# Adding spectral products on VectorE instead of TensorE in a two-layer SSM and GEGLU kernel, with a reordered opening

## The chip, the cores and the metric

The kernel runs on one core of a Trainium2 chip. The metric is the device time of one launch in microseconds (us). A core has five engines that run their own instruction lists and wait for each other through semaphores: TensorE (PE, with its weight loads shown as PEld), VectorE (DVE), ScalarE (ACT), GpSimd (POOL) and SyncE (SP). In this kernel the last two mostly issue DMA transfers; POOL also does small per-row statistics.

## The reference

One sequence of S = 2048 tokens with D = 576 features goes through two layers. Each layer has a gated long convolution (A) and a GEGLU feed-forward block (B), both with the same weights in both layers.

```python
def _A_ref(q, k, v, shift_k, ssm_k, ssm_D):
    ...                                   # k_shift: 4-tap causal filter of k
    kv = k_shift * v
    ...                                   # y: causal convolution of kv with ssm_k over 2048 tokens, by FFT
    y = y + kv * ssm_D[None, None, :]
    return q * y
def _B_ref(x, w_gate, w_up, w_down):
    return (_gelu(x @ w_gate) * (x @ w_up)) @ w_down    # 576 -> 4608 -> 576
x = A_q
x = x + _A_ref(_layernorm(x, axis=-1), A_k, A_v, A_shift_k, A_ssm_k, A_ssm_D)
x = x + _B_ref(_layernorm(x, axis=-1), B_w_gate, B_w_up, B_w_down)
x = x + _A_ref(_layernorm(x, axis=-1), A_k, A_v, A_shift_k, A_ssm_k, A_ssm_D)
x = x + _B_ref(_layernorm(x, axis=-1), B_w_gate, B_w_up, B_w_down)
```

The convolution depends on k, v and the filters alone, not on x. Its result y is computed once and used by both layers, as a gate on the normalised x.

## The kernel before

**Feed-forward part.** The tokens are cut into four chunks of 512 (c = 0 to 3), each of four tiles of 128 rows. A unit is a pair (layer, chunk). The units run in the order (0,0), (0,1), (1,0), (1,1), (0,2), (0,3), (1,2), (1,3), numbered 0 to 7, and are grouped in passes [0], [1,2], [3,4], [5,6], [7] (L711). A pass goes three times through a third of the 4608 hidden columns, for each of its units; one such step is called a visit here, and there are 24. A visit has 12 gate-up groups (L1087: 18 matmuls each of 64 rows by 512 columns into one PSUM pair from a pool of three; ACT takes the Gelu, L1091; DVE multiplies it with the up half into hT, L1092) and then four down groups (L1103: 24 full-array matmuls of 288 columns each; DVE adds the result to x_c, L1132 or L1137).

Before its first visit a unit's input has to be gated with y (L855 and L862, with row statistics on POOL, L819 to L835, and a square with row sum on ACT, L827), normalised (L888 and L890, tile xn) and transposed by DMA from SP's queue into xnT (L918, two transfers for each of the four tiles). Unit 0's input is transposed on PE in the opening instead (`turn0`, L1002).

**Convolution part.** It is done by blocks of 512 tokens in a frequency domain of 512 points, in four tiles of 128 frequencies (kt = 0 to 3) with two parts each, 0 and 1. H are the transformed filter blocks, K the transformed kv blocks. Block m of the result needs the products K[a] * H[m-a] for a = 0 to m. Each of them takes, for each kt and part, a multiplication (`prod`, L222 or L225) and a subtraction or addition (L226) on DVE, and gives a bf16 tile `sum` of 128 by 576. Blocks 1, 2 and 3 have 16, 24 and 32 such products. `accumulate` (L229) adds them up on PE: each product is the moving operand of two matmuls of 288 columns with an identity as weights, and the sum stands in PSUM (cps). For kt < 2 ACT copies it to an f32 tile eo (L391). For kt >= 2 `both` (L235) makes the sum and the difference of that tile and the PSUM one (L240), and `shifted` (L243, L245) combines these with the block before into z. Four inverse transforms (L258) then give the tiles of y. The forward transform of a kv block is L205, with ACT copies into eo (L208) and DVE sums (L213). The kv block itself is made by L160 to L170. K and H blocks are kept in DRAM (Kd, Hd): they are spilled by POOL's DMAs (L263) and read back into kr and hr buffers (L316, L324).

**What sets the order.** All lists are in program order. A planner in the kernel (`Pace`, with one constant per operation, L30 to L37, and `fill`, L973) places the convolution work among the visits while the program is built: after each gate-up group and within the down groups it takes operations from two VectorE queues, one of the convolution (`run_v`, L443) and one of gates and norms (`run_vq`), as long as its own clocks leave room, and PE's convolution work (`run_p`, L460). `hurry()` (L1049) is true until block 1's last inverse is placed. As long as it is, the convolution's queue goes first and PE's convolution work may stand between gate-up groups; later gates and norms go first, and that PE work stands within down groups only. `conv.spills` holds POOL's small operations and spills with the time from which they may be placed.

**The opening** (`begin`, L472) makes the DFT tables, the four H blocks in 16 tiles (`h_tile`, L567; matmuls L184, eviction by ACT L186, spill L263), block 0 of the convolution and unit 0's input. Most of H's tiles pass through the `hr` buffers, four before; the order of its last part is written out by hand (from L641).

Of the kernel before, what the change touches and what calls it, by code (L numbers as in the profile page):

```python
# [12 lines left out]
ALU = mybir.AluOpType  # L13
# [41 lines left out]
class Conv:  # L55
# [9 lines left out]
    def __init__(self, tc, ctx, pace, A_k, A_v, A_shift_k, A_ssm_k, A_ssm_D, ident, psp, cpsp, ypool):  # L65
# [10 lines left out]
        self.krp = pool("c_kr", 3)  # L76
        self.hrp = pool("c_hr", 4)
# [4 lines left out]
        self.eop = pool("c_eo", 2)  # L82
        self.kvp = pool("c_kv", 1)
# [15 lines left out]
        self.U = deque()  # L99
        self.kr_free, self.hr_free = [0.0] * 3, [0.0] * 4  # L100
        self.npr = self.nkr = self.nhr = 0
        self.V, self.L, self.Pq = deque(), deque(), deque()
        self.spills = deque()

# [167 lines left out]
    def step(self, m, kv=None, loaded=False):  # L272
# [37 lines left out]
        def load(kt, a):  # L310
            def run():
                if a < m:
                    kr[(kt, a)] = (self.nkr % 3, self.krp.tile([P, 2, D], BF16, tag="kr", name="kr"))
                    self.kr_free[self.nkr % 3] = NEVER
                    self.nkr += 1
                    nc.gpsimd.dma_start(out=kr[(kt, a)][1][:].rearrange("p s d -> p (s d)"), in_=self.Kd[a][kt])  # L316
                if m == 1 and a == 0:
                    hr[(kt, a)] = (None, self.H1[:, kt, :, :])
                    at[("ld", kt, a)] = t.pe + 8.0
                    return  # L320
                hr[(kt, a)] = (self.nhr % 4, self.hrp.tile([P, 2, D], BF16, tag="hr", name="hr"))
                self.hr_free[self.nhr % 4] = NEVER
                self.nhr += 1
                nc.gpsimd.dma_start(out=hr[(kt, a)][1][:].rearrange("p s d -> p (s d)"), in_=self.Hd[m - a][kt])  # L324
                at[("ld", kt, a)] = t.pe + 8.0
            return run
        for kt, a in pairs:
            self.L.append((lambda a=a: max(self.hr_free[self.nhr % 4] if (m, a) != (1, 0) else 0.0,
                                           self.kr_free[self.nkr % 3] if a < m else 0.0),
                           load(kt, a)))  # L330
# [25 lines left out]
        def v(kt, a, part):  # L356
            def run():
                K = kc[kt] if a == m else kr[(kt, a)][1]
                slot = self.npr % N_SM
                prs[(kt, a, part)] = (slot, self.prod(part, K, hr[(kt, a)][1]))  # L360
                self.pr_free[slot] = NEVER

# [7 lines left out]
                return fin  # L370
            return run
        for kt, a in pairs:
            for part in range(2):
                keys = [("ld", kt, a)] + ([("kc", kt % 2, s, h) for s in range(2) for h in range(2)] if a == m else [])
                self.V.append((lambda g=get(*keys): max(g(), self.pr_slot()), C_PR, v(kt, a, part)))
        st = {}

# [32 lines left out]
        for kt in range(2):  # L410
            for s in range(2):
                for h in range(2):
                    self.Pq.append((lambda: max(get("kv")(), NEVER if self.neo > 1 else 0.0), 0.49, fwd(kt, s, h)))
        for kt in KTS:
            for part in range(2):
                for a in range(m + 1):
                    need = get(("pr", kt, a, part))
                    self.Pq.append(((lambda need=need: max(need(), NEVER if self.neo > 1 else 0.0)) if kt < 2 and a == m
                                    else need, 0.245, acc(kt, part, a)))
# [23 lines left out]
    def run_v(self, limit):  # L443
# [9 lines left out]
        if r > t.pe + 0.2 or max(t.dve, t.pe - 1.0) + cost > limit:  # L453
            return False
        self.V.popleft()
        fin = run()
        fin(t.on_dve(cost, r))
# [13 lines left out]

    def begin(self, gate0, norm0, turn0, x0_stats, more, scratch, wide, stay):  # L472

        tc, nc, D = self.tc, self.nc, self.D
        with ExitStack() as es:
# [176 lines left out]
            inv0(3)  # L652
            nc.scalar.activation(out=warm[:], in_=self.pis[:, 1:2], func=ACT.Gelu_apprx_tanh)
            more(2)
# [27 lines left out]
            h_tile(3, 3, self.hrp)  # L682
# [6 lines left out]
def ssm_geglu_kernel(ctx, tc, A_q, A_k, A_v, A_shift_k, A_ssm_k, A_ssm_D, B_x, B_w_gate, B_w_up,  # L689
# [126 lines left out]
    def mean_after(v, when):  # L816
        def run():
            v["nm"] = small.tile([P, 1], F32, tag=v["pfx"] + "nm", name="nm")
            nc.gpsimd.tensor_scalar(out=v["nm"][:], in0=v["s"][:], scalar1=-1.0 / D, scalar2=None, op0=ALU.mult)  # L819
            v["nm_at"] = max(t.pe, when) + C_TINY  # L820
        conv.spills.append((when, run))

    def square_task(get_x, v):
        def run():
# [6 lines left out]
            def root():  # L831
# [4 lines left out]
                v["rstd_at"] = max(t.pe, when) + 2 * C_TINY  # L836
            conv.spills.append((when, root))
        aq.append((at_v(v, "nm_at"), C_SQ, run))
# [150 lines left out]
    with tc.manual_schedule():  # L989
# [11 lines left out]

        def turn0(j, act):  # L1002
            if 0 not in xnT_of:
# [3 lines left out]
            for b in range(NKC):  # L1007
                c0 = b * P if b < 5 else HK + (b - 5) * P
                nc.tensor.transpose(pt[:, b // 5, (b % 5) * P:(b % 5 + 1) * P], xn0[j][:, c0:c0 + P], ident[:])
            (nc.scalar.copy if act else nc.vector.tensor_copy)(  # L1010
                out=xnT_of[0][:, 5:NKC, tok], in_=pt[:, 1, 0:4 * P].rearrange("p (b q) -> p b q", q=P))
            nc.scalar.copy(out=xnT_of[0][:, 0:5, tok], in_=pt[:, 0, 0:5 * P].rearrange("p (b q) -> p b q", q=P))
# [3 lines left out]
        def gate0(j):  # L1016
# [3 lines left out]
            aq.pop()[2]()  # L1020
            conv.spills.pop()[1]()

        def more(k):
# [7 lines left out]
            else:  # L1031
                load_x(1)
        conv.begin(gate0, norm0, turn0, lambda k: [run() for _, _, run in g0[4 * k:4 * k + 4]], more,
                   lambda dt: xtp.tile([P, RT if dt == I32 else 2, D], dt, tag="xnT", name="ang"),
# [19 lines left out]
        for wb, ph, ui, first, final in visits:  # L1054
# [25 lines left out]
            for fi in range(FP):  # L1080
# [13 lines left out]
                if gi == FG - 1 and final:  # L1094
                    when_due(t.pe + (FP - FG) * C_GU + 12.0, load_wgu, n + 3)
                fill(t.pe + C_GU + LEAD, hurry(), hurry())
            for j in range(RT):
# [17 lines left out]
                for fi in range(FP):  # L1115
# [76 lines left out]
```

## Time and profile before

| | us |
|---|---|
| Median of three runs | 977.12 (976.35 to 979.27) |
| The profiled execution, its own time | 973.51 |
| Its span, first to last instruction | 971.7 |
| PE busy in it | 949.8 (98%) |
| DVE busy in it | 537.3 (55%) |
| ACT busy in it | 305.4 (31%) |
| First gate-up matmul | 65.82 |

The profile is one execution, in which each instruction has its start and duration. A row of groups names the source line, engine, operation, output and inputs, the shape and count, then the busy time and the mean of one in ns, then the engine's idle time just before these instructions and what ended it. The chain is the work that ended last, followed back from the last instruction. A row of stretches gives the length and each engine's busy time in it. An engine that is not on the chain may be idle for free, and its time counts only where another engine waits for it.

### The profile page before, as it was taken

The numbers are of one execution on the slowest core, as the hardware profiler recorded it, in microseconds if no ns is written. First come the engines' busy times: TensorE is split into PE (matmuls) and PEld (weight loads), VectorE is DVE, ScalarE is ACT, GpSimd is POOL, SyncE is SP. The second block draws the span as 40 slices with busy tenths as digits, with TensorE's granted clock in tenths as the row PEclk, the third lists the DMA queues.
The fourth block names the chain that finished last, engine by engine and source line by source line (L and its number), as shares of the span: only waits on it lengthen the run. The fifth ranks groups of instructions, "written<-read, shape, count | busy, mean of one in ns | idle before, by whom it ended". The sixth has DMA issues, their size and how long they took to land.

```text
span 971.7 us, 19304 instructions
## 1 busy us (share of the span) xinstructions
PE 949.8 (98%) x8256; PEld 547.9 (56%) x8256; DVE 537.3 (55%) x973; ACT 305.4 (31%) x559; POOL 139.5 (14%) x303
## 2 busy tenths in 40 slices
PE   8989999879999999999999999999999999999998
PEld 5755554536556465565565565565565466466455
DVE  8957887858498555879543333564323324533332
ACT  7765213522221533414113322233212213411211
POOL 2353100512020301413000000231000001200000
PEclk9999999989999999999999999999999999999999
DMA  7989975955680740497360270385360450398730
GB/s 180 307 227 291 271 171 134 181 150 123 128 281 22 152 121 14 110 209 189 81 155 16 45 148 30 74 145 125 68 152 1 88 133 1 54 239 170 158 77 26
DMA packets 129067, 127.48 MB, mean 131 GB/s; under 512 B 45588, under 2 KB 121685, under 8 KB 128981
## 3 DMA queue, kind: packets, MB, share of 16 engines
q1 hardware_dynamic: 119904, 90.85, 44.4%
q0 software_dynamic: 8944, 34.49, 11.0%
q8 instruction: 64, 1.05, 0.5%
q10 hardware_dynamic: 132, 0.91, 0.3%
q14 instruction: 23, 0.18, 0.1%
HBM read 105.58 MB, written 10.62 MB: 120 GB/s over the span
## 4 chain that ended last, share of the span: by engine, by line
PE 92%; DVE 4%; DMA 3%; ACT 1%; issue 0%; POOL 0%; ACTq 0%; SPq 0%; DVEq 0%
PE gu L1087 58%; PE dn L1103 28%; PE cps L232 2%; PE cps L258 1%; PE cps L205 1%; DMA k<-in_A_k_dram 1%; DMA xnT<-xn 1%; DMA Hd<-h 1%; DVE kvt L160 1%; PE ps L184 0%; DVE prod L225 0%; DVE yb L226 0%; DVE kvt L165 0%; PE ps L258 0%; DVE stats L771 0%
## 5 line engine op out<-in xcount | busy, mean ns | idle before, releaser
L1087 PE MATMUL gu<-xnT,wgu 64*128 64x512 bf16 x5184 | 568.2, 377 | 7.9 <-DMA xnT<-xn 7.9
L1087 PEld LDWEIGHTS <-wgu 64*128 64x128 bf16 x5184 | 251.4, 94 | 314.8 <-issue 19.3
L1092 DVE TENSOR_TENSOR hT<-ga,gu 128x512 bf16<-128x512 f32 x288 | 197.7, 687 | 282.4 <-ACT ga L1091 281.1
L1091 ACT ACTIVATE ga<-gu 128x512 f32<-128x512 f32 x288 | 171.9, 597 | 545.0 <-PE gu L1087 541.9
L1103 PE MATMUL dn<-wd,hT 128*128 128x288 bf16 x2304 | 297.4, 286 | 0.5 <-DVE ob L1112 0.5
L1103 PEld LDWEIGHTS <-hT 128*128 128x128 bf16 x2304 | 223.3, 98 | 66.4 <-issue 10.5
L1137 DVE TENSOR_TENSOR x_c<-x_c,dn 128x576 f32<-128x576 f32 x64 | 48.2, 753 | 83.2 <-PE dn L1103 82.8
L819 POOL TENSOR_SCALAR nm<-s 128x1 f32<-128x1 f32 x60 | 20.6, 343 | 370.4 <-DVE x_c L1132 160.2
L827 ACT ACTIVATE junk<-x_c,nm 128x576 bf16<-128x576 f32 x48 | 36.9, 769 | 22.2 <-POOL nm L819 22.1
L835 POOL TENSOR_TENSOR rstd<-ve,neghalf_t 128x1 f32<-128x1 f32 x60 | 36.9, 614 | 5.0
L226 DVE TENSOR_TENSOR sum<-prod 128x576 bf16<-128x576 bf16 x72 | 33.0, 458 | 2.7
L184 PEld LDWEIGHTS <-G 128*128 128x128 bf16 x256 | 25.9, 102 | 14.6 <-issue 5.7
L184 PE MATMUL ps<-h,G 128*128 128x288 bf16 x192 | 27.8, 299 | 4.2 <-ACT h L186 3.0
L324 POOL DMA_DIRECT2D hr<-Hd x32 | 17.4, 543 | 73.5 <-DVE prod L225 73.4
L1123 DVE TENSOR_TENSOR ob<-x_c,dn 128x576 bf16<-128x576 f32 x15 | 11.3, 754 | 29.4 <-PE dn L1103 18.4
L834 POOL TENSOR_SCALAR ve<-ss 128x1 f32<-128x1 f32 x60 | 17.7, 296 | 64.8 <-ACT junk L827 64.6
L316 POOL DMA_DIRECT2D kr<-Kd x24 | 13.7, 572 | 85.2 <-DVE prod L225 85.2
L232 PE MATMUL cps<-sum,ident 128*128 128x288 bf16 x144 | 25.3, 287 | 0.0
L160 DVE TENSOR_TENSOR kvt<-k,skc 128x1152 bf16<-128x1152 bf16 x32 | 23.9, 754 | 1.8 <-DMA k<-in_A_k_dram 1.2
L213 DVE TENSOR_TENSOR kc<-eo 128x288 bf16<-128x288 f32 x48 | 19.4, 452 | 2.7 <-ACT eo L208 2.6
L208 ACT COPY eo<-cps 128x576 f32<-128x576 f32 x24 | 15.3, 636 | 16.1 <-PE cps L205 11.9
L266 POOL DMA_DIRECT2D out_dram<-ob x12 | 6.7, 561 | 88.9 <-DVE ob L1123 88.9
(115 smaller groups left out, 471.3 us busy)
## 6 DMA issues: line engine op xcount, KB each, us to landing
wgu<-in_B_w_gate_dram SPq DMA_DIRECT2D x45, 576.0 KB, 5.8
wd<-in_B_w_down_dram SPq DMA_DIRECT2D x30, 864.0 KB, 7.3
wgu<-in_B_w_up_dram SPq DMA_DIRECT2D x45, 512.0 KB, 7.7
hr<-Hd POOLq DMA_DIRECT2D x32, 288.0 KB, 5.5
kr<-Kd POOLq DMA_DIRECT2D x24, 288.0 KB, 4.6
Hd<-h POOLq DMA_DIRECT2D x12, 288.0 KB, 4.2
Kd<-kc POOLq DMA_DIRECT2D x12, 288.0 KB, 8.1
k<-in_A_k_dram POOLq DMA_DIRECT2D x3, 1008.0 KB, 12.2
```

What stands on the lines that cost most here:

```text
L160: nc.vector.tensor_tensor(out=st[dst][:], in0=self.kt_[b][:, s0:s0 + 2, :], in1=self.skc[:, j, :].unsqueeze(1).to_broadcast([P, 2, D]), op ...
L184: nc.tensor.matmul(ps[:, h, 0:HW], lhsT=G[:, i, s * NFQ + kt * P: s * NFQ + (kt + 1) * P], rhs=src[:, i, h * HW:(h + 1) * HW], start=(i == ...
L226: nc.vector.tensor_tensor(out=dst, in0=pr[:, 0, :], in1=pr[:, 1, :], op=ALU.subtract if part == 0 else ALU.add)
L232: nc.tensor.matmul(ps[:, h, 0:HW], lhsT=self.ident[:], rhs=pr[:, h * HW:(h + 1) * HW], start=first, stop=last)
L819: nc.gpsimd.tensor_scalar(out=v["nm"][:], in0=v["s"][:], scalar1=-1.0 / D, scalar2=None, op0=ALU.mult)
L827: nc.scalar.activation(out=junk[:], in_=get_x(), func=ACT.Square, bias=v["nm"][:, 0:1], accum_out=v["ss"][:])
L835: nc.gpsimd.tensor_tensor(out=v["rstd"][:], in0=ve[:], in1=neghalf_t[:, 0:1], op=ALU.pow)
L1087: nc.tensor.matmul(pair[:, s, :], lhsT=w[r0:r0 + HK, k, gi * P:(gi + 1) * P], rhs=xnT[r0:r0 + HK, b, :], start=(k == 0), stop=(k == NKC - 1))
L1091: nc.scalar.activation(out=ga[:], in_=pair[:, 0, :], func=ACT.Gelu_apprx_tanh)
L1092: nc.vector.tensor_tensor(out=hT[:, fi, :], in0=ga[:], in1=pair[:, 1, :], op=ALU.mult)
L1103: nc.tensor.matmul(acc[:, h, 0:HW], lhsT=hT[:, fi, j * P:(j + 1) * P], rhs=wd[2 * wb + fi // WT][:, fi % WT, h * HW:(h + 1) * HW], start=( ...
L1137: nc.vector.tensor_tensor(out=xh, in0=xh, in1=acc[:, :, 0:HW], op=ALU.add)
```

## The change

For blocks 2 and 3 the identity matmuls go. The first product of each kt and part is written as f32 into a tile `zs` from the eo pool, each further one is added to it by an f32 `tensor_tensor` on DVE, and the sum and difference are then made from two such tiles in SBUF, without an ACT copy. Block 1 stays as it was. The pool of `sum` tiles shrinks from six to four, that of hr from four to three, and that of eo grows from two to four.

The order changes in three places. The convolution's VectorE queue goes first only until block 1's own operations are done (`conv.left`), where it was until its last inverse is placed. POOL's statistics may be placed two units of the planner's time earlier (`AHEAD`), at a smaller booked cost (`C_TINY`). In the opening the Gelu table is loaded earlier, and the gates of tiles 0, 2 and 1 and their statistics come before the H tiles that follow, with the last step of the statistics split off as `root0`; all four of unit 0's transposes are now evicted half by DVE and half by ACT.

```diff
-C_SQ, C_TINY = 0.85, 1.0
-N_KC, N_SM = 4, 6
+C_SQ, C_TINY = 0.85, 0.6
+N_KC, N_SM, N_EO, N_HR = 4, 4, 4, 3
+C_AC, C_AB = 0.65, 0.8
+AHEAD = 2.0
...
         def v(kt, a, part):
             def run():
                 K = kc[kt] if a == m else kr[(kt, a)][1]
+                if m > 1 and a == 0:
+                    sums[(kt, part)] = self.eop.tile([P, 2, HW], F32, tag="eo", name="zs")
+                    self.prod(part, K, hr[(kt, a)][1], sums[(kt, part)][:].rearrange("p h d -> p (h d)"))
+                else:
...
+        def add(kt, a, part):
+            def run():
+                slot, pr = prs[(kt, a, part)]
+                f = sums[(kt, part)]
+                nc.vector.tensor_tensor(out=f[:], in0=f[:], in1=self.halves(pr[:]), op=ALU.add)
...
+        def cross(kt, part):
+            def run():
+                b = self.both(kt, part, sums[(kt, part)][:], sums[(kt + 2, part)][:])
...
+                if m > 1:
+                    self.V.append((lambda: 0.0, C_AC, add(kt, a, part)))
+                    if a == m and kt >= 2:
+                        self.V.append((lambda: 0.0, 2 * C_AB, cross(kt - 2, part)))
+                        self.V.append((lambda: 0.0, 2 * C_TB, shift(kt - 2, part)))
...
-        for kt in KTS:
+        for kt in KTS if m == 1 else ():
             for part in range(2):
                 for a in range(m + 1):
...
             pair0(1, 0)
+            nc.scalar.activation(out=warm[:], in_=self.pis[:, 1:2], func=ACT.Gelu_apprx_tanh)
             h_tile(1, 1, self.hrp)
...
             inv0(3)
-            nc.scalar.activation(out=warm[:], in_=self.pis[:, 1:2], func=ACT.Gelu_apprx_tanh)
...
             gate0(0)
             gate0(2)
+            root0(0)
+            root0(2)
+            gate0(1)
+            root0(1)
             h_tile(2, 2, self.hrp)
+            norm0(0)
             h_tile(2, 1, self.hrp)
-            gate0(1)
-            norm0(0)
+            gate0(3)
+            root0(3)
+            norm0(2)
+            turn0(0)
             h_tile(2, 3, self.hrp)
-            turn0(0, True)
-            gate0(3)
-            norm0(2)
+            turn0(2)
+            norm0(1)
             h_tile(3, 0, self.hrp)
-            turn0(2, True)
-            norm0(1)
+            turn0(1)
+            norm0(3)
             kv1_ops(2)
             h_tile(3, 2, self.hrp)
-            norm0(3)
-            turn0(1, False)
-            kv1_ops(2)
+            turn0(3)
+            kv1_ops(6)
             h_tile(3, 1, self.hrp)
-            turn0(3, False)
-            kv1_ops(4)
             h_tile(3, 3, self.hrp)
...
-        conv.spills.append((when, run))
+        conv.spills.append((when - AHEAD, run))
...
         conv.step(1, kv=conv.kv1[8:], loaded=True)
+        conv.left = len(conv.V)
...
-                fill(t.pe + C_GU + LEAD, hurry(), hurry())
+                fill(t.pe + C_GU + LEAD, hurry(), conv.left > 0)
...
-                        fill(t.pe + 1.5, True, hurry())
+                        fill(t.pe + 1.5, True, conv.left > 0)
```

More of the change, by code (lines that the diff above doesn't have):

```diff
@@ L371, in v, with fin, shift, run @@
             return run
+        sums = {}
+        def add(kt, a, part):
[3 more added lines that the diff above has]
+                nc.vector.tensor_tensor(out=f[:], in0=f[:], in1=self.halves(pr[:]), op=ALU.add)
+                def fin(when):
+                    self.pr_free[slot] = when
+                return fin
+            return run
+        def cross(kt, part):
+            def run():
+                b = self.both(kt, part, sums[(kt, part)][:], sums[(kt + 2, part)][:])
+                for sg in range(2):
+                    nyb[(part, kt, sg)] = b[sg]
+                return lambda when: None
+            return run
+        def shift(kt, part):
+            def run():
+                for sg in range(2):
+                    z[(part, kt, sg)] = self.yb[(1 - part, kt, sg)]
+                    self.shifted(nyb[(part, kt, sg)], z[(part, kt, sg)], part)
+                return lambda when: mark(("z", kt, part), when + LAG)
+            return run
+        eo_done = get(*[("kc", kt, s, h) for kt in range(2) for s in range(2) for h in range(2)])
         for kt, a in pairs:
@@ L455, in run_v @@
         self.V.popleft()
+        self.left -= 1
         fin = run()
@@ L836, in root @@
                 v["rstd_at"] = max(t.pe, when) + 2 * C_TINY
-            conv.spills.append((when, root))
+            conv.spills.append((when - AHEAD, root))
         aq.append((at_v(v, "nm_at"), C_SQ, run))
@@ L1032, in more @@
                 load_x(1)
-        conv.begin(gate0, norm0, turn0, lambda k: [run() for _, _, run in g0[4 * k:4 * k + 4]], more,
+        conv.begin(gate0, root0, norm0, turn0, lambda k: [run() for _, _, run in g0[4 * k:4 * k + 4]], more,
                    lambda dt: xtp.tile([P, RT if dt == I32 else 2, D], dt, tag="xnT", name="ang"),
```

37 lines of the change are left out of this document (21 added, 16 removed).

## The prediction

> **What bounds the kernel now.** I read the page first (the chain by engine), then who TensorE waited for, then the chain in order of time, then stretches of the run.
>
> ```profile
> span 971.7 us, 19304 instructions
> ...
> PE 92%; DVE 4%; DMA 3%; ACT 1%; issue 0%; POOL 0%; ACTq 0%; SPq 0%; DVEq 0%
> ```
> ```profile
> PE gu L1087 <- DMA xnT<-xn: 7.9, 1, 7.9
> ```
> TensorE (PE) is the bound: 92% of the chain. Its only long wait is one of 7.9 us for the transposed input xnT of unit 1. It never waits for the gate product hT that VectorE (DVE) makes. So an instruction taken off PE shortens the run by its own spacing, unless something else becomes late.
>
> ```profile
> 544.18 23.41 PE gu L1087 x216
> 567.60 11.87 PE dn L1103 x96
> ```
> ```profile
> 146.60:191.60 45.00, 44.57 (x379) 25.49 (x378) 36.34 (x75) 20.23 (x38) 11.46 (x26) 1.00 0.70 152
> 191.60:199.50 7.90, 0.01 (x2) 0.04 (x2) 0.78 (x3) 0.00 (x0) 1.26 (x4) 0.80 1.15 272
> 199.50:238.70 39.20, 39.20 (x330) 21.63 (x332) 31.27 (x62) 12.10 (x24) 10.81 (x22) 0.95 0.54 133
> 199.50:506.90 307.40, 307.40 (x2688) 176.75 (x2690) 209.16 (x389) 90.36 (x168) 52.27 (x108) 0.99 0.55 129
> 276.10:314.90 38.80, 38.80 (x343) 22.55 (x344) 33.21 (x58) 8.07 (x14) 3.73 (x7) 1.00 0.35 122
> 430.70:468.50 37.80, 37.80 (x335) 21.77 (x336) 32.16 (x64) 11.57 (x22) 9.59 (x20) 1.00 0.76 186
> 544.20:579.50 35.30, 35.30 (x314) 19.77 (x316) 11.26 (x16) 12.82 (x28) 3.82 (x12) 1.00 0.55 103
> ```
> The second fence gives the spacing: 96 full-array matmuls of 288 columns in 11.87 us, 0.1236 us each. The third has one visit (one unit, one third of its hidden columns) to a row; its columns are length, then PE, PEld, DVE, ACT and POOL busy, granted clock, DMA share, GB/s. A visit with no convolution matmuls takes 35.30. The visit from 430.7 has 20 identity matmuls by the program's order and takes 2.5 more, 0.125 each: they sit among matmuls of their own shape and cost just their spacing.
>
> **The change part by part.**
>
> 1. *Identity matmuls removed.* Block 2 makes 24 products and block 3 makes 32, each added by two matmuls: 112. At 0.1236 us that is **-13.8 us**, all on the path. Nothing of it was hidden: in those visits PE is busy for the whole length.
>
> 2. *Adds on VectorE.* Eight of each block's products are now written in f32, and the other 40 each get an f32 add.
>
> ```profile
> L1092 DVE TENSOR_TENSOR hT<-ga,gu 128x512 bf16<-128x512 f32 x288 | 197.7, 687 | 282.4 <-ACT ga L1091 281.1
> ...
> L226 DVE TENSOR_TENSOR sum<-prod 128x576 bf16<-128x576 bf16 x72 | 33.0, 458 | 2.7
> ...
> L240 DVE TENSOR_TENSOR yb<-eo,cps 128x576 bf16<-128x576 f32 x24 | 17.0, 748 | 3.1 <-PE cps L232 3.0
> ...
> L222 DVE TENSOR_TENSOR prod<-kr,hr 128x1152 bf16<-128x1152 bf16 x20 | 15.0, 751 | 0.0
> ```
> No row has an all-SBUF f32 add of 576 elements. It lies between the bf16 form, 0.458, and the f32 form with one PSUM side, 0.748. I take 0.748, because its element size is that of the add: 40 x 0.748 = 29.9, and 16 x (0.748 - 0.458) = 4.6 for the f32 products, so DVE gets +34.5 us (18.3 at the low end). The 16 L240 operations stay and read SBUF; 8 ACT copies go, and ACT, with 1% of the chain, is no bound.
>
> Does it fit beside PE? The eight visits from 199.5 to 506.9 (307.4 us, the row above) hold 209.2 us of DVE work. They shrink to about 292 and then hold 244, 84% on average. The densest visit by the order of the changed program is the eighth: 12 hT products (8.2), 11 convolution products (each 0.751 for the multiplication and 0.458 for the sum or difference, 13.3, and 0.9 for three f32 forms), 8 adds (6.0) and 8 other f32 operations of 576 (at 0.748, 6.0) are about 34 us in 35.3, some 96%. The densest before were 33.21 of 38.80 (86%) and 32.16 of 37.80 (85%), without one PE wait on hT. The cover is three PSUM pairs: a late hT product stops PE only once it is over one gate-up group late. The planner books 0.65 for an add that I price at 0.748, so DVE falls behind its plan by 0.1 per add, 4 us over all, in two dense stretches. Below, nothing; above, those 4 us in full. I take **+1.0 us**, nearer to the rows that show no wait.
>
> 3. *Unit 1's gates first.* This aims at the 7.9 us.
>
> ```profile
> 189.58 9.22 DMA xnT<-xn
> ```
> ```profile
> 174.75 0.42 PE L1103 MATMUL dn<-wd,hT 128*128 128x288 bf16 x2
> ```
> ```profile
> 189.36 0.57 DVE L888 TENSOR_SCALAR xn<-x_c,nm,rstd 128x576 bf16<-128x576 f32 x1
> ```
> ```profile
> 183.19 11.48 SPq L918 DMA_TRANSPOSE xnT<-xn  x6
> ```
> Today the last normalised tile is made at 189.4, waits behind four other transposes on SP's queue, and has landed 9.2 us later, when PE has been through with unit 0 since 191.6. In the changed program VectorE's list leaves the convolution at the end of block 1: three tiles are normalised, and their six transposes issued, before this visit's down stage, and the fourth stands right behind the first down group (24 matmuls from 174.75, so 177.7, then 0.8 for its residual add and 0.8 for the norm: 179.5). SP has no weight load between these transposes. With the same 9.2 it lands at 188.7; PE needs it at 191.3. So the wait goes, with 2.6 us to spare, and so does what follows it: the visit at 199.5 took 39.20 where 35.30 and 16 matmuls of 0.12 make 37.2, at a granted clock of 0.95. Together 7.9 + 2.0 = **-9.9 us**; nothing if it stays. Next late would be unit 2's input, but its last transposes stand 14 us of PE work ahead of its use. The nm operations now go to POOL up to 2 us early, where they hold back the kr and hr loads queued behind them by at most as much.
>
> ```profile
> hr<-Hd POOLq DMA_DIRECT2D x32, 288.0 KB, 5.5
> kr<-Kd POOLq DMA_DIRECT2D x24, 288.0 KB, 4.6
> ```
> The planner books 8 us for these loads (a constant of the code), and they land in 5.5 and 4.6: the rest covers it, and I cost it at nothing; without that cover VectorE would wait those 2 us.
>
> 4. *The opening.* The Gelu table load moves ahead, the gates of tiles 0, 2 and 1 come first, and the H buffers shrink from four to three.
>
> ```profile
> 45.95 1.28 ACT L653 ACT_TABLE_LOAD   x1
> ...
> 58.86 1.19 ACT L186 ACTIVATE h<-ps 128x576 bf16<-128x576 f32 x2 [1.03 <-DMA Hd<-h]
> ```
> ```profile
> 51.92 6.86 DMA Hd<-h
> ...
> 63.42 0.50 PE xps L1009 x9
> 63.92 0.98 PE cps L184 x8
> ...
> 65.88 4.20 PE gu L1087 x37
> ```
> ```profile
> 50.81 1.14 PE L184 MATMUL cps<-h,G 128*128 128x288 bf16 x8 [1.65 <-ACT h L186]
> ```
> Tile (2,0) is spilled at 51.92 and lands at 58.8; only then can ACT evict the tile four places on, and PE runs without pause from 59.56 to the gates at 65.88. With three buffers the same landing releases the tile *three* places on, (2,3). The table load (1.28) no longer stands before the squares, but a third gate's statistics now go to POOL ahead of the spill: I take its issue at 50.9, one earlier. PE: from about 51.1 a transpose (0.50), two half tiles (0.98 each), a transpose and a half tile, to 55.1; then it waits. Landing 50.9 + 6.86 = 57.8, two evictions 1.2, PE again at 59.0; seven half tiles and two transposes are left, 7.9: gates at 66.9, **+1.1 us**. If the landing doesn't move (the DMA engines are what is full there), +2.1; if it takes the 2.4 of the later spills, no pause is left and the gates start at 55.1 + 7.9 = 63.0, -2.9.
>
> ```profile
> DMA to landing us min/median/max: 6.8/6.8/6.9
> ```
> ```profile
> DMA to landing us min/median/max: 2.4/2.4/2.4
> ```
> These are the two spills from 51.9, and that of 64.4. I take the first, being at the same place.
>
> The pause from 55.1 to 59.0 is longer than any in the opening now (1.65), all of which kept clock 1.00; the 7.9 pause was followed by 0.95 and a loss of 2.0. [...]
>
> **Sum.** -13.8 + 1.0 - 9.9 + 1.1 = -21.6 us. The profiled execution took 973.51 (span 971.7 and 1.8 around it) and would take 951.9. The median of the runs is 977.12, 3.6 above it; the same difference gives **955.5 us**.
>
> **The rivals.**
>
> - *The transposes still come late* (a slow landing, or DVE late with the fourth norm): 9.9 is not won: 965.4. For: only 2.6 us to spare, at DMA shares up to 1.15. Against: three of four tiles are long through. 0.11.
> - *VectorE late in the dense visits, mildly*: all 4 us of the planner's error and some late inverses, 6 in place of 1: 960.5. 0.12.
> - *VectorE becomes the bound, and the kernel slower.* Place: the seven visits of blocks 2 and 3 that hold adds, 84 gate-up groups, each with its hT behind an add in VectorE's queue. If each stopped PE by an add (0.748) it would cost 62.8, less 22.6: 1017. It decides from 22.6 / 84 = 0.27 us per group on. For: 96% busy. Against: no wait on hT at 86%, and the three PSUM pairs. 0.04.
> - *The clock falls in the opening's pause*: 2.0 more by the visit at 199.5: 957.5. [...] 0.10.
> - *The matmuls leave and PE waits instead*, say for weights, so that nothing is gained: 977. PE is busy over whole visits at DMA shares near 0.5. 0.02.
>
> **How the numbers follow.** My forecast, with small deviations, has 0.61; it is the likeliest. Lowest: no loss on VectorE and -2.9 in the opening, 977.1 - 26.6 = 950.5; with the runs' scatter of about one below the median, 949.5. The range reaches up over the mild rival, the clock and the late transposes, to 966; left out are the rest of these and the last two, about 0.12. About 0.3% (3 us) is what a measurement of this kernel tells from no change. Faster: 0.61 + 0.11 + 0.12 + 0.10 = 0.94; same 0.02; slower 0.04.
>
> **What would show it.** Step 1: 32 identity matmuls left, the fourth, fifth and eighth to tenth visits at 35.3 to 36. Step 2: the add's row near 750 ns, and no PE wait on hT over 1 us. Step 3: the wait on xnT gone from PE's list and clock 1.00 in the visit behind it. Step 4: one PE pause near 4 us, ended by ACT behind an Hd landing, gates starting near 67. I am wrong if PE lists many waits on hT, if the adds run far over 750 ns, or if a later unit's xnT wait appears.

## The result, and the profile after

The changed kernel took 953.67 us (median of four runs, 952.37 to 953.76) against 977.0 for the kernel before (976.35 to 979.27): a ratio of 0.9754, with a 95% interval from 0.9736 to 0.9772. 955.5 had been forecast, with a range of 949.5 to 966. The profiled execution is the one of 952.37, with a span of 950.6.

First the page of the changed kernel, then who PE waited for (us in total, times, longest), its head and seven of its rows:

```profile
span 950.6 us, 19103 instructions
...
PE 934.6 (98%) x8144; PEld 537.8 (57%) x8144; DVE 568.8 (60%) x1015; ACT 299.1 (31%) x549; POOL 141.0 (15%) x303
...
PE 92%; DVE 4%; DMA 2%; POOL 1%; ACT 1%; issue 1%; SPq 0%; DVEq 0%; ACTq 0%; POOLq 0%
```
```profile
PE xps L1057 <- ACT h L189: 3.2, 1, 3.2
PE ps L187 <- ACT h L189: 1.4, 2, 0.8
PE cps L208 <- ACT eo L211: 1.3, 1, 1.3
...
PE gu L1138 <- DVE ob L1174: 0.7, 1, 0.7
```

The bound is the same, PE with 92% of the chain. The wait for unit 1's xnT, 7.9 us before, is gone from the list; no wait for hT has come. A pause of 3.2 in the opening is new, and so is one of 1.3 behind an ACT copy in unit 0's last visit.

The visits, in stretches (length, then PE, PEld, DVE, ACT and POOL busy, granted clock, DMA share, GB/s):

```profile
192.90:228.20 35.30, 35.30 (x315) 19.78 (x316) 31.09 (x61) 9.62 (x19) 11.46 (x22) 1.00 0.94 213
228.20:263.50 35.30, 35.30 (x314) 19.78 (x316) 31.34 (x55) 7.17 (x12) 4.35 (x9) 1.00 0.71 159
263.50:302.70 39.20, 39.20 (x346) 22.89 (x346) 34.13 (x56) 9.77 (x16) 3.64 (x7) 1.00 0.38 139
...
341.90:377.20 35.30, 35.30 (x314) 19.79 (x314) 32.60 (x61) 10.64 (x20) 9.13 (x19) 1.00 0.40 134
377.20:412.40 35.20, 35.20 (x314) 19.68 (x313) 27.98 (x54) 10.18 (x20) 10.30 (x22) 1.00 0.76 145
412.40:448.60 36.20, 35.52 (x315) 21.30 (x316) 34.57 (x65) 10.29 (x20) 9.89 (x21) 1.00 0.76 179
```

The visits that only add now take 35.2 to 35.3, the length of one without convolution matmuls; the one of 39.20 holds inverse transforms. PE fills each of them except the last, where the 0.7 is the wait on ob. DVE is fullest in that one too, with 34.57 of 36.20.

The groups that answer to the removed matmuls and the added operations:

```profile
L385 DVE TENSOR_TENSOR zs<-zs,sum 128x576 f32<-128x576 f32 x40 | 30.2, 755 | 0.8
L229 DVE TENSOR_TENSOR zs<-prod 128x576 f32<-128x576 bf16 x16 | 12.1, 758 | 0.5
L243 DVE TENSOR_TENSOR yb<-zs 128x576 bf16<-128x576 f32 x16 | 11.4, 752 | 0.0
L235 PE MATMUL cps<-sum,ident 128*128 128x288 bf16 x32 | 6.1, 289 | 0.0
```

32 identity matmuls are left, those of block 1. The f32 forms take 0.752 to 0.758 each, where 0.748 was priced.

**Where the 21.1 us of the span come from.** The first gate-up matmul of the chain ("the gates" in what follows) moved from 65.88 to 66.70, so the opening lost 0.8. From the gates to the end it is 905.8 before and 883.9 after, 21.9 less: the xnT wait 7.9, 112 matmuls at 0.1236 or 13.8, the slow clock behind the wait about 1.9, together 23.6; against them stand the new waits on eo (1.3, which replaces one of 0.3) and on ob, the output tile (0.7). The chain shows where the 1.3 begins: POOL issues two Kd spills from 187.74 ahead of a tile's statistics, ACT's square waits for these until 190.32, and the eo copy stands behind the square, at 191.19. Neither the rule alone nor the two runs of the changed kernel without it (below) have this wait. In the experiments I compare this same stretch, because the opening of these kernels varies with its first transfer: PE waits 0.9 us for it in this profile and 3.7 in the first experiment's, where the opening's code is that of before.

### The profile page after: what moved, and what is told of

Its sections match the earlier page's. It is cut to its first block, busy times and chain, and to the rows that moved or that the text cites. A ratio compares the mean times of both kernels' runs of the same rounds, so it can differ in the third digit from the quotient of the medians.

```text
span 950.6 us, 19103 instructions
## 1 busy us (share of the span) xinstructions
PE 934.6 (98%) x8144; PEld 537.8 (57%) x8144; DVE 568.8 (60%) x1015; ACT 299.1 (31%) x549; POOL 141.0 (15%) x303
## 4 chain that ended last, share of the span: by engine, by line
PE 92%; DVE 4%; DMA 2%; POOL 1%; ACT 1%; issue 1%; SPq 0%; DVEq 0%; ACTq 0%; POOLq 0%
PE gu L1138 59%; PE dn L1154 28%; PE cps L261 1%; PE cps L208 1%; PE ps L187 1%; DMA out_dram<-ob 1%; DMA hn<-in_A_ssm_k_dram 1%; DMA Hd<-h 1%; PE cps L235 0%; DVE prod L228 0%; DVE yb L229 0%; DVE prod L225 0%; POOL rstd L883 0%; DVE yb L667 0%; DVE stats L819 0%
## 5 line engine op out<-in xcount | busy, mean ns | idle before, releaser
L1154 PE MATMUL dn<-wd,hT 128*128 128x288 bf16 x2304 | 292.0, 287 | 0.5 <-DVE ob L1163 0.5
L385 DVE TENSOR_TENSOR zs<-zs,sum 128x576 f32<-128x576 f32 x40 | 30.2, 755 | 0.8
L229 DVE TENSOR_TENSOR sum<-prod 128x576 bf16<-128x576 bf16 x56 | 25.7, 458 | 2.0
L168 DVE TENSOR_TENSOR kvt<-kvt 128x1152 bf16<-128x1152 bf16 x24 | 18.1, 755 | 0.4
```

Source lines behind the costliest of these rows:

```text
L229: nc.vector.tensor_tensor(out=dst, in0=pr[:, 0, :], in1=pr[:, 1, :], op=ALU.subtract if part == 0 else ALU.add)
L385: nc.vector.tensor_tensor(out=f[:], in0=f[:], in1=self.halves(pr[:]), op=ALU.add)
L1154: nc.tensor.matmul(acc[:, h, 0:HW], lhsT=hT[:, fi, j * P:(j + 1) * P], rhs=wd[2 * wb + fi // WT][:, fi % WT, h * HW:(h + 1) * HW], start=( ...
```

## The experiments

My theory after the result: the prediction's four steps hold, each with its own mechanism. The rivals to it were that the queue rule is not what removed the wait, that the adds are free only by luck of the planner's numbers, and that the opening works otherwise than described.

### The queue rule alone

```diff
 # kernel before
+        self.left -= 1
...
+        conv.left = len(conv.V)
...
-                fill(t.pe + C_GU + LEAD, hurry(), hurry())
+                fill(t.pe + C_GU + LEAD, hurry(), conv.left > 0)
...
-                        fill(t.pe + 1.5, True, hurry())
+                        fill(t.pe + 1.5, True, conv.left > 0)
```

> The kernel before, with one edit: VectorE's list leaves the convolution's queue as soon as block 1's own operations are done, not when its last inverse is placed. My theory: PE waited 7.9 us for unit 1's transposes and lost 2.0 more to the clock behind it; the last transposes now stand some 10 us of PE work earlier, so the wait goes: 977.0 - 9.9 = 967.1 us, no wait on xnT, the visit behind it at 37.2 us. Rival: the time is only moved, since the convolution of block 2 that gave way comes late for its own users: 975 to 977, with new PE waits on products or y. Second rival: the wait goes only with POOL's statistics booked earlier as well: about 972.

Measured: 965.32 against 975.75, ratio 0.9881 (0.9846 to 0.9916). PE's list has no xnT wait, and the mean clock is 1.00. From the gates to the end 895.7, so 10.1 less than before, where 9.9 was forecast for this step. Put into the kernel before, the rule does what it was priced at.

### The changed kernel without the rule

```diff
 # kernel after
-                fill(t.pe + C_GU + LEAD, hurry(), conv.left > 0)
+                fill(t.pe + C_GU + LEAD, hurry(), hurry())
...
-                        fill(t.pe + 1.5, True, conv.left > 0)
+                        fill(t.pe + 1.5, True, hurry())
```

> The changed kernel with that one edit undone; the identity matmuls stay away, the opening and the earlier statistics stay. Their booking alone puts unit 1's last transposes 2.9 us of PE work earlier than in the kernel before. My theory: the wait shrinks by that, to about 5 us, and the clock falls behind it again by up to 2.0: 953.7 + 7 = 960.7 us. Rival: the transposes' landing is set by the DMA load at that place and not by their issue: a wait of 7.9 again, 963.5. Second rival: the earlier statistics were what removed the wait: 953.7.

Measured: 956.18, ratio 0.9792 (0.9759 to 0.9826), less than the 960.7 expected. PE waits 3.3 us for xnT, not 7.9, and from the gates to the end it is 887.0, only 3.1 more than with the rule. So 7 of the 10 us are won without the rule. The wait of before had more than one part; the next two runs look for them.

### The adds and the opening, without the rule and the earlier statistics

```diff
 # kernel after with the rule undone as above, and
-C_SQ, C_TINY = 0.85, 0.6
+C_SQ, C_TINY = 0.85, 1.0
-AHEAD = 2.0
+AHEAD = 0.0
```

> The changed kernel without the queue rule and without the earlier statistics: the adds on VectorE and the opening alone. The fourth norm of unit 1 then stands 2.8 us of PE work earlier than in the kernel before, 3.7 later than in the run with only the rule undone, whose wait on xnT was 3.3 us. My theory: the wait goes with the place of that norm: about 5 us, with up to 2.0 for the clock: 958 to 960. Rival: the adds alone, which free SP and PE at that place, shortened the wait: 3.3 again, 956. Second rival: both edits are needed to get anything: 7.9 and the clock, 963.5.

The changed kernel ran beside it once more:

> The changed kernel itself on this chip, to set the others against: 951 to 954 us.

Measured: 953.64 (950.81 to 954.48), ratio 0.9758 (0.9727 to 0.9789); the changed kernel in the same comparison 952.28 (951.24 to 952.88), ratio 0.9746 (0.9717 to 0.9774). From the gates to the end 882.6, the shortest of all. That is against my expectation: nothing of the queue rule is in it, and there is no xnT wait. SP's queue shows a part of the reason. Below are the kernel before, up to its six transposes from 183.19 that the prediction shows, then this one (start, length, operation):

```profile
178.14 2.54 SPq L918 DMA_TRANSPOSE xnT<-xn  x2
180.78 0.62 SPq L745 DMA_DIRECT2D wgu<-in_B_w_gate_dram  x1
...
182.13 0.63 SPq L747 DMA_DIRECT2D wgu<-in_B_w_up_dram  x1
```
```profile
181.14 11.46 SPq L966 DMA_TRANSPOSE xnT<-xn  x8
192.70 0.61 SPq L793 DMA_DIRECT2D wgu<-in_B_w_gate_dram  x1
...
194.45 0.69 SPq L795 DMA_DIRECT2D wgu<-in_B_w_up_dram  x1
```

Before, three weight loads go ahead of six of the eight transposes, and POOL sends x_b (a later chunk's input rows) at 189.47; here the weights go behind the transposes, and x_b leaves at 193.78. These are the times from issue to landing of the six before:

```profile
DMA to landing us min/median/max: 7.1/7.8/8.0
```

The chain's piece of 9.22 is the sixth transpose, issued at 189.58, whose landing this view leaves out; it belongs to the third tile. The last tile's two were issued at 191.36 and 192.80 and landed 7.9 and 7.1 us later, the first of them at 199.29; PE went on at 199.49. Here they were issued at 189.96 and 191.23 and landed 3.5 and 2.8 us later, and PE starts on xnT at 193.74 without a wait.

The last norm starts at nearly the same time in both traces, 189.36 and 189.14, but the gates do not (65.88 and 69.09). Counted from the gates the norm is 3.4 us earlier here (120.1 in place of 123.5), and PE is through with unit 0 at 124.7 in place of 125.7. So the tile has 2.4 us more before PE needs it, and from the start of its norm to its first landing it takes 4.4 us in place of 9.9. Both parts together, 2.4 and 5.5, are the wait of 7.9. In the run above, with the earlier statistics and without the rule, the weights stand between the transposes again (from 183.13).

### The weight loads behind the transposes

```diff
 # kernel before
-        while due:
+        while due and not 0 < xn_done.get(1, 0) < RT:
```

> The kernel before, with one thing moved on SP's queue: the three wgu weight loads that stand between unit 1's second and third transposes (issued at 180.78 to 182.76 in the profile of before) go behind its last transpose; every other engine's list is the same, and no operation is added or left out. Theory (the transposes land late because that megabyte of weights is on the DMA engines ahead of them, and not because the last norm is late): the last normalised tile at 189.4 is followed by its transposes at once and lands about 2.5 us after their issue, at 193.8, where it landed at 198.8; the wait of PE for xnT goes from 7.9 to 2 to 3 us, and the visit behind it takes 37.2 to 38 in place of 39.2: 5.5 to 7.5 us off, about 970 where before is 976 to 977 (ratio 0.992 to 0.994). Rival (the norm's time sets it, or other traffic holds the transposes back anyway): the landing stays at 5 to 9 us, the wait at 5 or more, the time within 3 us of before; then the queue rule's ten microseconds come from the earlier norms alone. A second rival: the moved loads are themselves late, and PE waits on wgu for what is gained.

Measured: 973.84 against 976.46, ratio 0.9975 (0.9961 to 0.9989), the theory's 970 missed. The chain's piece for xnT, which here is the last transpose from its issue to its landing, and PE's wait are:

```profile
191.43 6.79 DMA xnT<-xn
```
```profile
PE gu L1087 <- DMA xnT<-xn: 6.2, 2, 5.6
```

The last tile's transposes were issued at 190.18 and 191.43, some 1.2 to 1.4 us earlier than before, and took 6.8 each, where it was 7.9 and 7.1: they landed 2.3 and 1.7 us earlier. The wait went from 7.9 to 6.2, in two pieces. A new wait of 0.8 on ob takes back a part, so that the profiles have 905.1 from the gates to the end against 905.8; between the medians it is 2.6. The rival has most of it: without the weight loads the transposes still take far more than 2.5, with x_b (issued at 189.48) and two Kd spills (from 190.82) on the DMA engines.

Here are the times of the last tile's two transposes from issue to landing, lined up by what was issued shortly ahead of or beside them:

| Run | transfers beside them | us to landing |
|---|---|---|
| the rule alone | none | 2.5 (the second; the trace has no landing of the first) |
| the adds and the opening | Kd spills | 3.5, 2.8 |
| the changed kernel without the rule | weights, two Kd spills | 4.5, 3.8 |
| block 1's adds (below) | x_b | 4.9, 4.2 |
| this run | x_b, two Kd spills | 6.8, 6.8 |
| before | weights, x_b, Kd spills | 7.9, 7.1 |

So the landing goes with the traffic, and with no single transfer. Only the weights were moved by themselves, and from 192.83 they are issued behind the transposes, still beside them in time. What x_b or a spill is worth alone is not shown.

Beside x_b, which is on POOL's queue, the transposes of SP's queue took 4.9 and 4.2 in place of 2.5, though x_b isn't ahead of them in any list. How the queues share the DMA engines is not shown.

### The old opening in the changed kernel

The edit undoes the last hunk of the diff (the order of the opening, `root0`, the early Gelu table, the evictions of the transposes) and keeps three hr buffers.

> The changed kernel with the opening's order of before (gates, statistics, Gelu table, transposes), but three H buffers as in the changed kernel. My theory: with three buffers the landing of the first spill (issued near 51.9, landed near 58.8) releases the tile three places on; PE then resumes near 60.0 with 8.4 us of work ahead of the gates, which start near 68.4 where the changed kernel has 66.6: 955.5 us. Rival: the reordering is itself what the opening lost: gates at 65.8 as before, 952.9.

Measured: 958.51, ratio 0.9817 (0.9787 to 0.9846); gates at 71.56, and 883.6 from there to the end, as in the changed kernel. PE's rows of this opening, then its clock in slices of 4 us:

```profile
60.15 2.08 PE L187 MATMUL ps<-h,G 128*128 128x288 bf16 x8 [6.08 <-ACT h L189]
62.03 1.16 PE L1054 MATMUL xps<-ident,xn 128*128 128x128 bf16 x9
62.99 2.12 PE L187 MATMUL cps<-h,G 128*128 128x288 bf16 x8
```
```profile
54.00:58.00 4.00, 0.07 (x1) 0.00 (x0) 2.09 (x4) 0.08 (x1) 2.31 (x4) 1.00 1.09 291
58.00:62.00 4.00, 1.85 (x8) 1.13 (x8) 0.00 (x0) 3.09 (x7) 0.00 (x0) 0.66 0.06 22
62.00:66.00 4.00, 4.00 (x23) 2.85 (x22) 0.76 (x2) 2.85 (x5) 2.04 (x4) 0.50 0.39 146
```

With three buffers and the old order PE stands for 6.1 us, and then its matmuls take twice as long (eight in 2.08, where 1.14 is usual) for about 6 us, 2.9 us lost by the starts of the rows. So the new order is what makes three buffers bearable; the gates at 68.4 that I expected left out the clock. It fell during the pause of 6.1 (0.63 from 59 to 60 us, 0.50 from 60 to 66); in other runs it fell with a pause of 3.16, and in one with 2.03 (last section).

### The adds doubled, with and without the planner's knowledge

```diff
 # kernel after
-                nc.vector.tensor_tensor(out=f[:], in0=f[:], in1=self.halves(pr[:]), op=ALU.add)
+                for _ in range(2):
+                    nc.vector.tensor_tensor(out=f[:], in0=f[:], in1=self.halves(pr[:]), op=ALU.add)
 # in the second run also
-C_AC, C_AB = 0.65, 0.8
+C_AC, C_AB = 1.5, 0.8
```

> The changed kernel with each of the 40 f32 adds issued twice, without telling the planner; the output then holds sums with these products doubled. 30 us more on VectorE. My theory: VectorE hides work as long as a visit has room for it; the fifth and eighth visits then hold 36.6 and 38.6 us of it in 35.3, and a lag of over one gate-up group reaches PE: 2 to 5 us longer, 956 to 959, with PE waits on hT or on y. Rival: every add stands in front of an hT that PE waits for: 30 us longer, 984. Second rival: VectorE is far from the bound: 953.7.

> The kernel with every f32 add issued twice (sums with doubled products), now with the planner told of 1.5 us per pair in place of 0.65. The untold one was 14 us longer than the changed kernel, with PE waits on hT. My theory: what it lost was room in single visits, not room over all: the eight visits hold some 274 us of VectorE work in 290, and the planner puts the adds further apart (block 2's result comes about 30 us later by its order, before it is needed): 1 to 5 us longer than the changed kernel, 955 to 959, few waits on hT. Rival: VectorE's work itself no longer fits, and the loss stays near 14: 967.

Measured: 967.7, ratio 0.9912 (0.9881 to 0.9942), with the planner untold, well over the 956 to 959 expected; 953.53, ratio 0.9776 (0.9753 to 0.98), with the planner told. The waits of PE in the first:

```profile
PE gu L1139 <- DVE hT L1144: 4.8, 6, 1.2
PE xps L1058 <- ACT h L189: 3.2, 1, 3.2
PE dn L1155 <- DVE hT L1144: 2.5, 4, 1.2
PE gu L1139 <- DVE ob L1175: 2.2, 2, 2.0
```

In the second no wait on hT stands in the list, though it has the same 80 adds (60.4 us); the last of them starts at 533.4, not 487.4. From the gates to the end it is 897.9 in the first and 884.3 in the second, against 883.9. So 30 us more on DVE cost 14.0 when they come unannounced into full visits, and 0.4 in this profile when the planner spreads them over later ones (the ratios, 0.9776 against 0.9754 for the changed kernel, leave room for some 2). So DVE is not near its limit over the run. What decides is whether an added operation is booked at its length: 40 adds booked 0.1 short cost at most the 0.7 on ob, 40 pairs booked 0.86 short cost 14.

### Block 1's adds on VectorE too

```diff
 # kernel after
-                if m > 1 and a == 0:
+                if a == 0:                       # and likewise at the two other places
-        for kt in KTS if m == 1 else ():
+        for kt in ():
```

> The changed kernel with block 1's products added on VectorE too: 32 more identity matmuls and 4 ACT copies go, 8 f32 adds and 8 f32 products come into the first three visits, which hold 33 to 39 us of VectorE work in 38 to 43. By PE alone it is 32 x 0.1236 = 4.0 us shorter. My theory: block 1's result comes later, the last transposes of unit 1 are placed only some 4 us of PE work before their use, and a part of the wait on xnT comes back, 1 to 3 us: 951 to 953. Rival: VectorE has the room here too, all 4.0 are won: 949.7. Second rival: it is full, and PE waits on hT as with the adds done twice: over 955.

Measured: 954.59, ratio 0.9785 (0.9765 to 0.9805), over the 951 to 953 expected. The last 32 identity matmuls, 4.0 us, are gone, and a wait of 7.9 on xnT is back:

```profile
PE gu L1138 <- DMA xnT<-xn: 7.9, 1, 7.9
```

PE is through with unit 0 at 182.7 here, or 114.5 after the gates where the changed kernel has 126.2: the identity matmuls are gone, 32 of block 1's forward matmuls (another 4.0) have moved behind this point, and the wait of 1.3 on eo is not there; the rest of the 11.7 is open. The last norm starts at 182.5, and its two transposes land at 190.5 and 191.1, 4.9 and 4.2 after their issue. That landing is not among the slow ones, but PE is early: matmuls that are taken from in front of a wait only make it longer. Behind the wait the clock is at 0.50 for 5.7 us more (190.6 to 196.3), and the visit's gate-up groups take 26.39 where 23.41 is usual; the run's mean clock is 0.992, that of the changed kernel 0.998. So from the gates to the end it is 886.7, 2.8 more than in the changed kernel.

### The opening's spills

```diff
 # early_spill: kernel after
+            self.flush(0.0)                  # spill of tile (2,0) issued before the gates
             gate0(0)
 # spill_first: that, and gate and root of tile 1 moved behind h_tile(2, 1)
 # spills_first: that, and another self.flush(0.0) ahead of them
```

> The changed kernel with one line more: the spill of H tile (2,0) is placed on POOL ahead of the three gates' statistics. In the changed kernel it left at 52.0 and landed at 57.4, and only then could ACT evict the tile three places on. My theory: that landing holds the opening; it now comes near 48, PE goes on after its first pause until it needs the next landing (the spill of (2,2), near 59.2), and the gates start near 65.5 where they started at 66.6: 1.1 us gained, 952.5. Rival: the clock's dip and the third gate's statistics hold the opening, and the landing only ended last by chance: gates at 66.6 again, 953.7.

> As the run with the early spill, and the gate of tile 1 moved back behind the H tiles (2,2) and (2,1), so that ACT evicts these right after the second gate's square. My theory: PE's first pause (3.2 us in the changed kernel, with the clock at 0.76 and 0.82 behind it) shrinks below 2 us, the clock stays at 1.00, the second spill leaves near 50 in place of 52, and the gates start between 62.5 and 64: 3 us gained, 950.5. Rival: gate 1's later normalisation delays the third transpose and PE waits there: gates at 65.5, no more than the early spill alone.

> As spill_first, with the spill of H tile (2,1) too placed on POOL ahead of the statistics of gates 1 and 3. In spill_first that spill left at 56.5 behind them, landed at 63.0 and held ACT for 2.9 us and PE for 1.9. My theory: each spill queued behind statistics on POOL is what holds the opening with three buffers; it now leaves near 51.5, the 1.9 go, and the gates start some 2 us earlier than in spill_first against the end of y's eviction: 950.3 us. Rival: the landing is set by the DMA load up to 60, whatever the issue: no change against spill_first, 952.2.

Measured: 951.15, ratio 0.9753 (0.9731 to 0.9775); 952.17, ratio 0.9757 (0.9736 to 0.9779), where 950.5 was expected; 949.38, ratio 0.9723 (0.9697 to 0.9749). The first rows below are ACT, POOL's spill and PE in the changed kernel's opening, with the granted clock in two slices; then PE and the clock in the third of these runs.

```profile
50.15 0.77 ACT L875 ACTIVATE junk<-x_c,nm 128x576 bf16<-128x576 f32 x1 [1.99 <-POOL nm L867]
...
52.04 1.16 POOL L266 DMA_DIRECT2D Hd<-h  x2
...
52.14 1.12 PE L1057 MATMUL xps<-ident,xn 128*128 128x128 bf16 x9 [3.16 <-ACT h L189]
53.05 2.13 PE L187 MATMUL cps<-h,G 128*128 128x288 bf16 x8
...
57.44 0.65 ACT L189 ACTIVATE h<-cps 128x576 bf16<-128x576 f32 x1 [2.48 <-DMA Hd<-h]
...
58.68 1.14 PE L187 MATMUL ps<-h,G 128*128 128x288 bf16 x8 [0.84 <-ACT h L189]
```
```profile
50.00:54.00 4.00, 1.86 (x13) 1.52 (x13) 1.96 (x6) 3.51 (x7) 2.39 (x6) 0.76 1.04 212
54.00:58.00 4.00, 3.84 (x30) 2.79 (x29) 1.07 (x3) 1.52 (x5) 1.34 (x3) 0.82 1.06 291
```
```profile
51.93 0.68 PE L1059 MATMUL xps<-ident,xn 128*128 128x128 bf16 x9 [0.68 <-DVE xn L1047]
54.30 2.23 PE L187 MATMUL ps<-h,G 128*128 128x288 bf16 x16 [1.70 <-ACT xnT L1061]
```
```profile
50.00:54.00 4.00, 1.93 (x20) 1.33 (x18) 3.44 (x9) 2.06 (x5) 1.88 (x6) 1.00 0.94 223
54.00:58.00 4.00, 3.69 (x35) 2.95 (x35) 0.91 (x2) 3.60 (x7) 1.67 (x3) 1.00 1.06 300
```

The changed kernel pauses twice: 3.16 us for ACT, which waits for POOL's statistics, and 0.84 for the spill's landing. The first pause halves the clock, but part of that time PE would have waited for the landing anyway. With the spill issued at 42.51 the second pause goes and the first stays; the gates come 1.3 earlier, counted from the pause's end. Moving tile 1's gate as well breaks up the first pause and holds the clock at 1.00, but ACT then waits 2.9 for the next spill, issued at 56.47, and about 1 us is won in place of 3. These two gains are read from the profiles alone: the ratios, 0.9753 and 0.9757, are those of the changed kernel (0.9754 and 0.9746). With that spill ahead of the statistics too, ACT's wait for it shrinks to 1.0 and PE's pause behind it goes: gates at 63.58 against 67.61 for the changed kernel in the same comparison, the rest of the run equal (883.5 both). The medians of that comparison differ by 2.9, and the slowest run of this version (950.80) is below the fastest of the changed kernel (951.24). It beats both kernels.

## Why the prediction was right, step by step

1. **The identity matmuls**, -13.8: right. The visits named came to 35.2 to 36.2.
2. **The adds**: the price of 0.748 was right within 1.5%, though the 0.752 to 0.758 measured lie just above the two rows that it was put between; the fullest visit was the tenth, not the eighth (which held 32.60 us where I had estimated about 34), and on the path there is at most the 0.7 on ob, where +1.0 was taken. The wait of 1.3 on eo stood in no step: ACT was taken to be no bound, and that statistics queued behind spills on POOL could hold an eviction was not followed. The rival with VectorE as the bound was rightly thought small, but my reason, the three PSUM pairs, was only half of it: doubling the adds showed that it is the planner's room in later visits that carries them.
3. **Unit 1's gates first**, -9.9: the size is right. The last norm started at 179.40 and was done at 180.2, where 179.5 was forecast for its end. The account is wrong in two respects. The 9.2 was misread: it is the third tile's second transpose, and the last tile waited on SP's queue behind that one, not behind four; its own two took 7.9 and 7.1. And I took the landing as given and the norm's time as what had to change. The runs show that the landing itself is 2.5 to 7.9, by the traffic around it. In the changed kernel the last one took 2.5 and was there at 184.0, 8.9 before PE came at 192.9, where 2.6 to spare was forecast. The adds and the opening without the rule are enough as well, by a norm that is 2.4 earlier against PE's need and a landing that is shorter. The rule removes the wait by itself, and so does the rest of the change without the earlier statistics; together they are not worth twice as much.
4. **The opening**, +1.1: measured +0.8, by another way. I expected one pause of 4 us behind the landing. There were two, of 3.2 and 0.8, and the longer one came from ACT waiting for POOL's statistics, which I had moved ahead in the sum but not followed to PE. The spill was issued at 52.04, not 50.9, and landed after 5.3, not 6.9; the errors cancelled. The rival of the falling clock did come true, at a cost of about 1.6 us of slower matmuls (by their starts from 52.14 to 56.19), most of it hidden under the wait for the landing. No run shows the chance of 0.10 that I gave it: a pause of 3.15 or 3.16, shorter than the 3.9 that I expected, came with the fall in four of the five profiles whose clock was read in slices around it (0.76, 0.77, 0.87 and 0.87 from 50 to 54 us; the fifth, without the rule, kept 1.00 from 47.02 to 57.26).

The sum of 21.6 met 21.1 in the profiles and 23.3 between the medians. The profiled execution of before was 3.6 us faster than the median of its first three runs, that of after 1.3 faster than its own; why the first is so much stays open.

## What to carry to other kernels

When the bound engine waits for a transfer, look at what else the DMA engines are given in the microseconds before, on every queue, and not only at when the transfer's data was ready: the same two transposes took from 2.5 to 7.9 us here. When an operation moves from the bound engine to one with room, tell whatever plans the order its true length: booked, 30 us cost 0.4 here, unbooked they cost 14. Work taken off the bound engine just ahead of a wait for data can be given back in the wait: with block 1's adds moved, 4.0 us of matmuls went, and a wait of 7.9 came.

## What I had not expected of the hardware

PE's clock was at half after a pause of 3.16 us, and in one run after a pause of 2.03. In slices of 1 us the changed kernel's clock is:

```profile
51.00:52.00 1.00, 0.00 (x0) 0.00 (x0) 0.57 (x2) 1.00 (x4) 0.82 (x2) 1.00 1.12 258
52.00:53.00 1.00, 0.86 (x9) 0.86 (x9) 0.00 (x0) 1.00 (x3) 1.00 (x3) 0.52 1.13 192
...
54.00:55.00 1.00, 1.00 (x6) 0.64 (x5) 0.00 (x0) 0.96 (x3) 0.46 (x2) 0.50 1.13 191
55.00:56.00 1.00, 1.00 (x8) 0.73 (x7) 0.00 (x0) 0.00 (x0) 0.88 (x2) 0.77 1.19 234
56.00:57.00 1.00, 1.00 (x15) 0.90 (x14) 0.10 (x1) 0.00 (x0) 0.00 (x0) 1.00 1.05 399
```

It is at half for 3.4 us and back at full before 56. The same pause of 3.16 in `early_spill` did it too (0.77 and 0.80 in its slices of 4 us), while a pause of 1.70 in `spills_first` left the clock at 1.00. Before, after 7.9 us, the half rate lasted from about 196.4 to 203.2, nearly half of it while PE stood still anyway.

The length of the pause alone does not decide. The first three rows below are the changed kernel without the rule, around its pause of 3.16 (48.81 to 51.97), which left the clock at 1.00; the other two are the adds done twice with the planner untold, around a pause of 2.03 (420.68 to 422.71):

```profile
47.02:50.43 3.41, 1.79 (x15) 1.29 (x14) 2.85 (x7) 1.32 (x3) 2.76 (x6) 1.00 1.26 187
50.43:53.85 3.42, 1.88 (x21) 1.60 (x21) 1.40 (x5) 3.07 (x7) 2.28 (x5) 1.00 1.00 196
53.85:57.26 3.41, 2.23 (x24) 1.75 (x22) 1.09 (x3) 0.95 (x3) 1.34 (x3) 1.00 1.13 222
```
```profile
420.24:423.65 3.41, 1.38 (x16) 0.62 (x12) 1.71 (x4) 0.60 (x1) 0.54 (x1) 1.00 1.11 231
423.65:427.06 3.41, 3.21 (x18) 1.22 (x16) 3.38 (x6) 0.60 (x1) 0.75 (x2) 0.50 1.09 307
```

In the first run PE stands for 1.6 and 1.5 us of the pause in two rows of 3.41 us, in the second for all 2.03 in one; other cuts would share the pauses differently. The half rate lasted 3.41 us in the changed kernel (52.04 to 55.46) and 6.83 before (196.37 to 203.20), by the clock records of the two traces, and about 6.8 in the old opening and with the weight loads behind, by slices of 1 us. What sets these lengths, and what besides the length of a pause decides whether the clock falls, is not shown.
